# Two more tiles turned by TensorE, three small loads moved to other queues, and the instruction order searched anew

## The chip, the core and the metric

The kernel runs on one core of one Trainium2 chip. A core has five engines that run side by side and wait for each other through semaphores: TensorE (PE, matrix products and transposes), VectorE (DVE), ScalarE (ACT), GpSimd (POOL) and SyncE (SP, which here only issues transfers). Transfers between the chip's memory (HBM) and the core's memory (SBUF), and transposes inside SBUF, are carried out by 16 DMA engines; SP, ACT and POOL each feed them through a queue of their own. Products are summed in PSUM, eight banks of 512 float32 values per partition. The metric is the device time of one execution, in microseconds.

## The reference

The input x is (1, 2048, 640) in bfloat16. Two branches work on the normalised x, and both are added to x itself:

```python
x  = A_x
xn = layernorm(x)                                  # over the 640 columns, no weights
X  = rfft2(xn, axes=(-2, -1)) * (w_r + 1j * w_i)   # 2048 x 321 complex filter
A  = irfft2(X, s=(2048, 640)).astype(bfloat16)
h  = gelu(xn @ w1 + b1)                            # 640 -> 1536, tanh approximation
B  = h @ w2 + b2                                   # 1536 -> 640
return x + A + B
```

## The kernel before

The 2048 rows are held as 16 tiles of 128 rows (row 16p + c is partition p of tile c). For each tile VectorE takes statistics (`bn_stats` on two halves of 320 columns, L651; `bn_aggr`, L653), GpSimd raises the variance to the power -1/2 (L655), and VectorE normalises (L673).

The dense branch needs the normalised tile turned, with the 640 columns on the partitions. Tiles named in `BYDMA` are turned by a DMA transpose that SP issues (L680); the others by five TensorE transposes with the identity matrix (L692) into a PSUM bank, from which VectorE or ScalarE copies them to `xnT` (L547, L548). Layer one is done in seven blocks of one, one, two, two, two, four and four tiles (`BLOCKS`), each in twelve column groups of 128: five products over the 640 columns into one PSUM bank, then gelu with bias on ScalarE (L742) into `gT`. W1 is loaded in three parts that hold column groups 0 to 2, 3 to 6 and 7 to 11 (`W1P`). The bias b1 is turned to a column by one small TensorE product with the identity (L638 copies the result). Layer two is four times three column groups, each 640 wide, for each tile. For the tiles in `KEEP` it is done early: the sum is taken out of PSUM by VectorE (L911, "kps") and added to x + b2, which waits in SBUF; for the others it is done at the end, in the same PSUM bank as the last product of the filter branch ("fps").

The filter branch is a two-dimensional Fourier transform by products with tables. VectorE folds two tiles at a time (L704, L708), a product with `gtab` transforms along the rows in steps ("aps"), products with `etab` transform the width in six groups ("bps"), small 32 x 32 products with `mtab` finish the rows ("cps"), VectorE multiplies by the filter (L809 with w_r or w_i, L813 to sum), and small products with `ntab` ("dps"), DMA transposes of the result (L834) and products with `getab` ("eps") go back. VectorE unfolds (L859, L864), and a last product with `htab` is added to layer two in PSUM; VectorE adds x + b2 (L920), and SP stores the tile (L923). x + b2 is made by a ScalarE copy of b2 (L887) and a GpSimd DMA that adds x to it (L905). That DMA waits for all loads of the filter and for the transposes of x.

The filter is loaded in 18 pieces: eight direct ones and ten mirrored ones of 16, 15 or 1 rows. Two of the direct ones are issued by GpSimd.

The order of the work is written out. Every operation has a number in the order in which the program creates it, and `ORDER` lists, for each engine, the numbers in the order in which the engine runs them. Each engine runs its list strictly in order and stops at an operation whose inputs or whose buffers aren't ready. The class `Sched` replays the lists against a small model of durations (`mm_us`, `dve_us`, `LAG` and others) only to give out PSUM banks and SBUF buffers and to place the semaphores; `PRIO`, `FOLD`, `GP`, `CHAIN` and `WAVE` belong to the search that made the lists, and some of them set dependences: `WAVE` says how many of the last transposes a reload of x waits for.

At the start, TensorE runs idle products on zeros (`WARM`: 42 at once, 12 more between the first transposes and layer one). The identity is loaded by GpSimd, b1 and the first part of W1 by ScalarE, and the rest by SP.

Of the kernel before, what the change touches and what calls it, by code (L numbers as in the profile page):

```python
# [9 lines left out]
ACT = mybir.ActivationFunctionType  # L10
# [79 lines left out]

def mm_us(n):
    return max(n / 2400.0 + 0.0027, 0.0265)
# [24 lines left out]
class Pool:  # L117
# [34 lines left out]
    "sp": """8 10 14 15 16 17 18 27 50 46 24 20 19 25 23 149 151 30 45 162 164 42 28 29 38 175 177 31 188 190 36 32  # L152
26 37 33 40 41 39 217 47 34 48 49 44 219 202 43 204 35 521 522 523 520 544 545 546 51 547 570 568 569 571 595 594
593 592 621 658 648 638 612 694 675 710 720 685 730 756 765 747 782 798 791 805""",
    "pe": """7 52 112 114 115 236 230 231 120 233 118 237 234 245 246 248 249 275 276 284 285 269 270 278 279 239 242 243 240 272 266 273
# [8 lines left out]
728 760 761 754 762 745 763 785 786 787 780 792 793 788 789 794 795 796 799 800 801 802 803""",  # L164
    "act": """11 12 13 53 116 232 121 238 235 247 250 277 286 271 280 244 241 274 268 292 256 253 134 137 283 301 265 130 328 131 322 307
# [3 lines left out]
566 563 574 573 587 457 460 466 478 475 463 469 757 597 598 481 472 624 783 748 660 661 696 732 733 767""",  # L169
    "dve": """0 54 55 56 59 58 111 60 113 117 122 123 119 66 63 62 65 64 67 124 126 125 132 135 127 138 139 69 70 72 73 71  # L170
# [5 lines left out]
662 664 665 697 698 693 699 779 701 700 674 735 768 734 709 736 737 719 769 684 770 729 772 755 771 764 746 781 790 797 804""",  # L176
    "pool": """3 1 2 9 4 57 61 68 75 82 89 96 5 103 22 21 6 110 604 630 677 650 739 640 667 774 712 722 614 784 749 758
687 703""",
# [21 lines left out]
ROW_NS = {256: 26, 384: 22, 512: 27, 640: 33, 642: 70, 768: 37, 1024: 47, 1280: 56, 1600: 68, 2560: 103, 4096: 160, 10272: 750, "acc": 152}  # L200
TAIL = 0.9
LAG = 1.6
# [5 lines left out]
class Sched:  # L208
# [38 lines left out]
    def schedule(self):  # L247
        free = {e: 0.75 for e in self.engines}
        dma_free = 0.0
# [29 lines left out]
        while left:  # L279
# [38 lines left out]
            t, e, o = best  # L318
# [8 lines left out]
            if o.nbytes:  # L327
                n, size = o.rows
                ring = rings[e]
                free[e] = ring.issue_end(t, dur, n)  # L330
                done = max(t + ring.lead, free[e] - dur + ring.lead, dma_free) + n * ROW_NS[size] / 1e3
                if e == "pool" and size == 256:
                    done = t + ring.lead + 0.6
                    dma_free += n * ROW_NS[size] / 1e3
                else:
                    dma_free = done
                ring.held.append((done, n))
                o.end = done + TAIL + (LAG if 8.0 < t < 60.0 and o.engs[0][0] != "pool" and size != 256 else 0.0)
            else:
                o.end = t + dur + LAT[e]  # L340
# [98 lines left out]
BYDMA = tuple(range(4, 16))  # L439
# [3 lines left out]
PRIO = {"hps": 30.0, "gelu": 46.5, "pb": 53.0, "pc": 64.0, "filt": 77.5, "ipc": 53.5, "eps": 47.0, "fin": 46.5}  # L443
AHEAD = 1
CHAIN = "b1 b0 c00 c01 b2 c10 d01 c11 d00 b3 b4 d11 c21 d10 c20 b5 c31 d21 d20 c30 d30 d31".split()
XASPLIT = ["01 234", "01 234", "01234", "01234", "01234", "01 234", "01 23 4", "01 234"]
KEEP = (0, 2, 3, 4, 5, 6, 9, 10, 11, 14)
HOME = tuple(sorted((KEEP + tuple(c for c in range(16) if c not in KEEP))[-8:], key=lambda c: (c not in KEEP, c)))
FOLD = (1.3, 1.8, -3.7, 28.8, -1.2, 39.3, 36.8, -1.2)
GP = (-43.0, 20.0, 8.0, 14.0, -28.0, 2.0, -14.0)  # L450
G1 = 0
WAVE = (0, 4, 0, 0, 0, 1, 0, 4, 2, 2, 3, 0, 2, 1, 1, 2)
WARM = (42, 12)


def bass_parallel_sum__spectral_gfnet__dense_activation_gelu__prompt_kernel(
# [21 lines left out]
    with ExitStack() as es:  # L478
# [51 lines left out]
        def load(dst, src, buf, rows, after=(), q="sp", issue=0.46, prio=400, gate=(), late=0.0):  # L530
            return K.op([(q, 0.7 if q == "pool" else issue)], prio, lambda e, _: e.dma_start(dst, src), writes=[buf], after=after, rows=rows, gate=gate, late=late)  # L531
# [50 lines left out]
        def load_w1(j, q="sp"):  # L582
            a, b = W1P[j]
            load(view(W1, 128 * a, [[F, 5], [1, 128 * (b - a)]]), w1v[:, :, 128 * a:128 * b], B_w1s[j], (40, 256 * (b - a)), q=q)
        load_x(0, 1)
        load(ident[:], const["I"], B_id, (8, 256), q="pool", prio=96, late=1.25)
        load_x(1, 1)
        load(b1t[:], b1v, B_b1, (1, 256), q="act", prio=410)
        load_w1(0, q="act")
        K.op([("act", 1.3)], 390, lambda e, _: e.preload_act_table(ACT.Gelu_apprx_tanh), writes=[Buf("table")], gate=[K.ops[-1]])  # L590
# [372 lines left out]
```

## Time and profile before

| | |
|---|---|
| time, three runs | 149.53, 150.71, 151.38 us (median 150.71) |
| the profiled execution | 150.96 us, its span 148.9 us |
| TensorE busy | 140.9 us, 95% of the span, 1755 products recorded |
| VectorE, ScalarE, GpSimd busy | 109.0, 85.8, 23.0 us |
| DMA | 23.68 MB in 32122 packets, mean 159 GB/s |
| granted TensorE clock | 1.00 |

The span is the time from the first to the last recorded instruction of the core; what the execution takes beyond it, 2.06 us, lies around it. "Busy" is the time in which at least one instruction of the engine runs; for TensorE the ends are modelled, and some records are missing. "PEld" is the loading of the stationary operand, which overlaps the products. A row of the timeline gives start and length in microseconds, the engine, the line of the program, what is written from what, the shape and the count of merged instructions, and in brackets the idle time ahead of it with what ended it. "SPq" and "ACTq" rows are the issuing of transfers, not the transfers. The answer for one tile ends with the time from issue to landing.

### The profile page before, as it was taken

The numbers are of one execution on the slowest core, as the hardware profiler recorded it, in microseconds if no ns is written. First come the engines' busy times: TensorE is split into PE (matmuls) and PEld (weight loads), VectorE is DVE, ScalarE is ACT, GpSimd is POOL, SyncE is SP. The second block draws the span as 40 slices with busy tenths as digits, with TensorE's granted clock in tenths as the row PEclk, the third lists the DMA queues.
The fourth block names the chain that finished last, engine by engine and source line by source line (L and its number), as shares of the span: only waits on it lengthen the run. The fifth ranks groups of instructions, "written<-read, shape, count | busy, mean of one in ns | idle before, by whom it ended". The sixth has DMA issues, their size and how long they took to land.

```text
span 148.9 us, 4190 instructions
## 1 busy us (share of the span) xinstructions
PE 140.9 (95%) x1755; PEld 92.4 (62%) x1772; DVE 109.0 (73%) x232; ACT 85.8 (58%) x159; POOL 23.0 (15%) x38
## 2 busy tenths in 40 slices
PE   7599989999979999999999999999999999999993
PEld 7599979989537554436654544554447656665572
DVE  1699799999843369759945967796102999997992
ACT  3179998899957869889655442303378640350000
POOL 3302220305200027100240002020020380000000
PEclk9999999999999999999999999999999999999999
DMA  4999999898999948904939664944624099521243
GB/s 121 342 390 317 357 102 209 209 237 201 270 177 166 173 86 176 255 13 99 158 61 164 124 165 92 89 87 92 131 45 88 4 226 262 189 76 44 88 144 127
DMA packets 32122, 23.68 MB, mean 159 GB/s; under 512 B 20440, under 2 KB 28760, under 8 KB 31976
## 3 DMA queue, kind: packets, MB, share of 16 engines
q1 hardware_dynamic: 29024, 17.32, 53.2%
q0 software_dynamic: 2400, 5.61, 17.1%
q10 hardware_dynamic: 680, 0.49, 1.1%
q8 instruction: 14, 0.23, 0.7%
q14 instruction: 4, 0.03, 0.1%
HBM read 13.58 MB, written 2.62 MB: 109 GB/s over the span
## 4 chain that ended last, share of the span: by engine, by line
PE 78%; DMA 7%; SPq 5%; ACT 4%; DVE 2%; issue 2%
PE ps L536 78%; DMA X<-in_A_x_dram 7%; SPq L531 5%; ACT gT L742 2%; ACT XV L547 1%; DVE stats L651 1%; DVE T L708 1%; ACT X L887 0%; DVE T L704 0%; DVE W L920 0%; DVE mv L653 0%
## 5 line engine op out<-in xcount | busy, mean ns | idle before, releaser
L536 PE MATMUL ps<-W,gT 128*128 128x128 bf16 (+3 forms) x380 | 54.8, 292 | 2.6 <-issue 1.1
L536 PE MATMUL ps<-xnT,W 128*128 128x256 bf16 (+2 forms) x420 | 57.1, 288 | 0.0
L536 PEld LDWEIGHTS ps<-W,gT 128*128 128x128 bf16 x396 | 29.8, 98 | 24.0 <-issue 2.2
L536 PEld LDWEIGHTS ps<-xnT,W 128*128 128x128 bf16 x420 | 34.8, 98 | 15.4 <-issue 1.2
L742 ACT ACTIVATE gT<-ps,b1col 128x256 bf16<-128x256 f32 (+2 forms) x84 | 37.9, 508 | 9.2 <-PE ps L536 9.0
L651 DVE BATCH_NORM_STATS2 stats<-X 128x6 f32<-128x320 bf16 x32 | 13.9, 475 | 3.3 <-DMA X<-in_A_x_dram 3.3
L905 POOL DMA_DIRECT2D X<-in_A_x_dram x8 | 7.0, 1126 | 51.4 <-DMA Wf<-in_A_w_i_dram 15.3
L859 DVE TENSOR_TENSOR Wf<-Wf 128x960 bf16<-128x960 bf16 (+1 forms) x12 | 7.1, 595 | 9.7 <-ACT Wf L547 9.5
L547 ACT ACTIVATE Wf<-ps 128x960 bf16<-128x960 f32 (+1 forms) x9 | 7.6, 880 | 11.2 <-PE ps L536 11.0
L809 DVE TENSOR_TENSOR T<-Y,Wf 128x1288 bf16<-128x1288 bf16 x16 | 12.4, 825 | 1.3 <-ACT Y L547 1.3
L547 ACT ACTIVATE Y<-ps 128x644 bf16<-128x644 f32 x11 | 7.5, 705 | 6.4 <-PE ps L536 6.4
L547 ACT ACTIVATE XV<-ps 128x512 bf16<-128x512 f32 (+2 forms) x12 | 9.7, 830 | 2.5 <-PE ps L536 2.5
L655 POOL TENSOR_TENSOR rstd<-mv,mhalf 128x2 f32<-128x2 f32 (+1 forms) x9 | 6.3, 704 | 29.6 <-DVE mv L653 24.5
L905 POOL DMA_DIRECT2D xnT<-in_A_x_dram x8 | 7.3, 1296 | 17.4 <-DMA XV<-U 9.6
L547 ACT ACTIVATE U<-ps 128x512 bf16<-128x512 f32 (+1 forms) x10 | 3.8, 434 | 9.3 <-PE ps L536 9.3
L547 ACT ACTIVATE Xb<-ps 128x960 bf16<-128x960 f32 (+1 forms) x7 | 7.6, 1108 | 2.7 <-PE ps L536 2.7
L708 DVE TENSOR_TENSOR T<-T 128x512 bf16<-128x512 bf16 (+1 forms) x32 | 8.3, 306 | 0.1
L920 DVE TENSOR_TENSOR W<-ps,xnT 128x640 bf16<-128x640 f32 (+2 forms) x10 | 6.8, 690 | 2.1 <-PE ps L536 1.8
L548 DVE CAST Xb<-ps 128x960 bf16<-128x960 f32 (+1 forms) x5 | 5.8, 1169 | 2.8 <-PE ps L536 2.8
L536 PE MATMUL ps<-getab,XV 32*128 32x160 bf16 (+1 forms) x128 | 7.5, 241 | 0.0
L548 DVE CAST Y<-ps 128x644 bf16<-128x644 f32 x5 | 4.1, 827 | 4.4 <-PE ps L536 4.4
L536 PEld LDWEIGHTS ps<-getab,XV 32*128 32x128 bf16 (+1 forms) x128 | 6.5, 146 | 1.3
(51 smaller groups left out, 134.8 us busy)
## 6 DMA issues: line engine op xcount, KB each, us to landing
X<-in_A_x_dram POOLq DMA_DIRECT2D x8, 320.0 KB, 4.0
xnT<-in_A_x_dram POOLq DMA_DIRECT2D x8, 320.0 KB, 5.3
out_dram<-W SPq DMA_DIRECT2D x15, 160.0 KB, 1.8
X<-in_A_x_dram SPq DMA_DIRECT2D x7, 320.0 KB, 9.7
W<-in_B_w_dram SPq DMA_DIRECT2D x4, 480.0 KB, 6.2
Wf<-in_A_w_i_dram SPq DMA_DIRECT2D x6, 160.5 KB, 6.3
Wf<-in_A_w_r_dram SPq DMA_DIRECT2D x6, 160.5 KB, 5.3
W<-in_B_w_dram SPq DMA_DIRECT2D x1, 800.0 KB, 8.8
```

The lines of the kernel that those rows point to most:

```text
L531: return K.op([(q, 0.7 if q == "pool" else issue)], prio, lambda e, _: e.dma_start(dst, src), writes=[buf], after=after, rows=rows, gate=g ...
L536: ins = e.matmul(o_, lhsT=lw, rhs=rh, start=st, stop=sp_, skip_group_check=True)
L547: return e.activation(dst(), src(), ACT.Copy, scale=scale)
L548: return e.tensor_copy(dst(), src())
L651: st_op[c] = K.op([("dve", 0.393)], pr, lambda e, _, c=c, h=h: e.bn_stats(stats[:, c, 6 * h:6 * h + 6], view(X, c * D + H2 * h, [[1, H2]]) ...
L655: K.op([("pool", 0.65)], 500, lambda e, _, a=a, b=b: e.tensor_tensor(out=rstd[:, a:b], in0=mv[:, a:b, 1], in1=mhalf[:, a:b], op=ALU.pow), ...
L708: ring_ops.append(K.op([("dve", dve_us(4 * w, 2))], pr, lambda e, _, op=op, x1v=x1v, xfv=xfv, o_=o_, o0=o0, o1=o1, w=w: e.tensor_tensor(ou ...
L742: K.op([("act", act_us(128 * nt, 1))], pr + PRIO["gelu"] + GP[bi], lambda e, _, c0=c0, nt=nt, fc=fc, hps=hps: e.activation(gT[:, fc, 128 * ...
L809: filt_ops.append(K.op([("dve", dve_us(4 * KP, 2))], pr, lambda e, _, k=k, Y=Y, TB=TB, pair=pair: e.tensor_tensor(out=view(TT, TB.slot * 8 ...
L859: K.op([("dve", dve_us(320 * n, 2))], pr + 2, lambda e, _, k=k, op=op, yo=yo, y2=y2, n=n: e.tensor_tensor(out=view(Wf, Y2 + y2.slot * 3 * ...
L905: xo_ops[c] = K.op([("pool", 0.9)], 51 - c / 20, lambda e, _, c=c, xov=xov: e.dma_start(xov(0, D), xv[:, c, :], accum_op=ALU.add), reads=[ ...
L920: K.op([("dve", dve_us(w))], 95, lambda e, _, os_=os_, fps=fps, o0=o0, w=w, xov=xov, base=base: e.tensor_tensor(out=view(W1, OST + os_.slo ...
```

## The change

Tiles 4 and 5 leave `BYDMA`, so TensorE turns six tiles instead of four, and DMA ten instead of twelve. The identity is loaded through ScalarE's queue, created behind the load of the gelu table, and b1 stays on that queue; the first part of W1 goes to SP's queue, so that all three parts are issued there, behind x tiles 0 and 1. The table load no longer has to follow the first part of W1. Of the idle products there are 38 and 12. `KEEP` loses tiles 4 and 14 and gains tile 8, so that nine tiles are kept. The cost model gets a lag by time of issue and by row size instead of one figure, and the search has been run again: every list of `ORDER` is new, and with two DMA transposes gone and ten TensorE transposes and two copies added, the numbers behind 145 are shifted.

```diff
+def lag(t, size):
+    if size == 256 or size == "acc":
+        return 0.0
+    if t >= 16.0 and size in (642, 10272):
+        return 0.3
+    return ([0.0] + [v for t0, v in LAG if t >= t0])[-1]
...
-    "sp": """8 10 14 15 16 17 18 27 50 46 24 20 19 25 23 149 151 30 45 162 164 42 28 29 38 175 177 31 188 190 36 32
-26 37 33 40 41 39 217 47 34 48 49 44 219 202 43 204 35 521 522 523 520 544 545 546 51 547 570 568 569 571 595 594
+    "sp": """8 12 13 14 15 16 17 18 19 25 20 43 28 46 32 31 24 23 27 33 37 164 166 29 48 179 190 177 192 38 49 42
+30 44 40 39 203 205 219 217 36 34 35 47 26 45 41 524 523 548 522 547 545 521 546 569 572 571 50 51 570 595 596 594
...
-LAG = 1.6
+LAG = ((1.6, 1.1), (3.9, 2.8), (16.0, 1.6), (60.0, 0.0))
...
-BYDMA = tuple(range(4, 16))
+BYDMA = tuple(range(6, 16))
...
-AHEAD = 1
+AHEAD = 3
...
-KEEP = (0, 2, 3, 4, 5, 6, 9, 10, 11, 14)
+KEEP = (0, 2, 3, 5, 6, 8, 9, 10, 11)
...
-G1 = 0
-WAVE = (0, 4, 0, 0, 0, 1, 0, 4, 2, 2, 3, 0, 2, 1, 1, 2)
-WARM = (42, 12)
+G1 = 1
+WAVE = (0, 3, 0, 0, 2, 0, 0, 4, 0, 2, 0, 2, 4, 2, 2, 3)
+WARM = (38, 12)
...
-        load(ident[:], const["I"], B_id, (8, 256), q="pool", prio=96, late=1.25)
+        K.op([("act", 1.3)], 420, lambda e, _: e.preload_act_table(ACT.Gelu_apprx_tanh), writes=[Buf("table")])
+        load(ident[:], const["I"], B_id, (8, 256), q="act", prio=410)
+        load(b1t[:], b1v, B_b1, (1, 256), q="act", prio=405)
         load_x(1, 1)
-        load(b1t[:], b1v, B_b1, (1, 256), q="act", prio=410)
-        load_w1(0, q="act")
-        K.op([("act", 1.3)], 390, lambda e, _: e.preload_act_table(ACT.Gelu_apprx_tanh), writes=[Buf("table")], gate=[K.ops[-1]])
+        load_w1(0)
         load_w1(1)
```

What the new lists do, in words. SP: x tiles 0 and 1, the three parts of W1 with x tiles 2 and 3 ahead of the third, `gtab`, x tiles 4 and 5, 6 and 7, 12 and 13, 8 and 9, a filter piece, x tiles 14 and 15, three small items, x tiles 10 and 11; b2 comes behind the first part of W2, `getab` and `htab` between the last transposes. The transposes of tiles 12 to 15 stand ahead of seven last loads, among them the fourth part of W2 and two mirrored pieces of w_i. ScalarE: b1, the table load, the identity, then copies and gelus; its first copy of b2 comes behind the last eviction of the row transform. GpSimd: its two filter loads are issued between the powers of the early tiles, the first of them waiting for x tiles 6 and 7. TensorE: all 50 idle products first, then the ten transposes of tiles 0 and 1, then layer one; layer two begins behind the third group of the width transform. VectorE: one half of tile 1's statistics ahead of tile 0's mean, tile 1's normalising ahead of the copy of tile 0; the product with w_i for the first pair ahead of the copy of the third group of the width transform.

More of the change, by code (lines that the diff above doesn't have):

```diff
@@ L151 @@
 ORDER = {
[L152 to L155 removed]
[8 rows of a table removed]
[L164 to L165 removed]
[3 rows of a table removed]
[L169 to L170 removed]
[5 rows of a table removed]
[L176 to L178 removed]
+    "sp": """8 12 13 14 15 16 17 18 19 25 20 43 28 46 32 31 24 23 27 33 37 164 166 29 48 179 190 177 192 38 49 42
+30 44 40 39 203 205 219 217 36 34 35 47 26 45 41 524 523 548 522 547 545 521 546 569 572 571 50 51 570 595 596 594
+593 622 613 658 649 639 675 685 694 757 731 711 766 748 721 782 798 791 805""",
+    "pe": """115 7 52 114 112 120 118 231 234 235 270 232 237 238 273 274 271 267 268 279 280 282 283 285 286 276 243 277 240 244 241 246
[8 rows of a table added]
+709 763 776 746 777 764 719 778 792 785 779 786 787 780 788 793 789 794 795 796 799 800 801 802 803""",
+    "act": """11 9 10 116 121 53 236 233 275 272 239 269 281 284 287 278 245 242 248 251 260 293 263 296 135 254 130 299 131 132 326 323
[3 rows of a table added]
+758 568 578 577 588 592 749 482 476 473 464 467 470 783 774 479 599 625 660 661 696 697 733 734 768 769""",
+    "dve": """0 55 54 58 56 59 60 111 117 113 119 122 123 127 63 62 65 66 64 67 124 125 126 133 136 140 139 138 143 141 142 144
[5 rows of a table added]
+657 663 665 664 638 698 648 699 693 701 700 674 684 735 736 737 738 770 756 730 710 765 720 771 772 773 747 781 790 797 804""",
+    "pool": """3 1 2 57 5 61 68 21 75 6 4 22 82 89 96 103 110 605 723 631 641 677 667 703 713 740 750 615 651 687 784 775
+759""",
 }
@@ L248, in schedule @@
         free = {e: 0.75 for e in self.engines}
-        dma_free = 0.0
+        dma_free = dma_last = 0.0
         rings = {"sp": Ring(1.05, 140), "act": Ring(1.05, 140), "pool": Ring(1.7, 200)}
@@ L330, in schedule @@
                 free[e] = ring.issue_end(t, dur, n)
-                done = max(t + ring.lead, free[e] - dur + ring.lead, dma_free) + n * ROW_NS[size] / 1e3
-                if e == "pool" and size == 256:
-                    done = t + ring.lead + 0.6
+                turn = size == 256 and n == 40
+                done = max(t + ring.lead, free[e] - dur + ring.lead, dma_last if turn else dma_free) + n * ROW_NS[size] / 1e3
+                dma_last = max(dma_last, done + lag(t, size))
+                if e == "act":
+                    done = t + ring.lead + 0.5
                     dma_free += n * ROW_NS[size] / 1e3
@@ L337, in schedule @@
                 ring.held.append((done, n))
-                o.end = done + TAIL + (LAG if 8.0 < t < 60.0 and o.engs[0][0] != "pool" and size != 256 else 0.0)
+                o.end = done + TAIL + lag(t, size)
             else:
@@ L442 @@
         "eps": [(0, 4)], "fin": [(4, 8), (0, 4)], "fps": [(4, 8)], "tps": ANY, "aps": ANY}
-PRIO = {"hps": 30.0, "gelu": 46.5, "pb": 53.0, "pc": 64.0, "filt": 77.5, "ipc": 53.5, "eps": 47.0, "fin": 46.5}
-AHEAD = 1
-CHAIN = "b1 b0 c00 c01 b2 c10 d01 c11 d00 b3 b4 d11 c21 d10 c20 b5 c31 d21 d20 c30 d30 d31".split()
-XASPLIT = ["01 234", "01 234", "01234", "01234", "01234", "01 234", "01 23 4", "01 234"]
-KEEP = (0, 2, 3, 4, 5, 6, 9, 10, 11, 14)
-HOME = tuple(sorted((KEEP + tuple(c for c in range(16) if c not in KEEP))[-8:], key=lambda c: (c not in KEEP, c)))
-FOLD = (1.3, 1.8, -3.7, 28.8, -1.2, 39.3, 36.8, -1.2)
-GP = (-43.0, 20.0, 8.0, 14.0, -28.0, 2.0, -14.0)
-G1 = 0
-WAVE = (0, 4, 0, 0, 0, 1, 0, 4, 2, 2, 3, 0, 2, 1, 1, 2)
-WARM = (42, 12)
+PRIO = {"hps": 23.0, "gelu": 27.0, "pb": 67.5, "pc": 50.5, "filt": 84.0, "ipc": 36.0, "eps": 80.0, "fin": 28.5}
+AHEAD = 3
+CHAIN = "b1 b0 c01 c00 b2 c10 d01 c11 d00 b4 b3 d10 d11 c20 c21 b5 c30 d20 d21 c31 d30 d31".split()
+XASPLIT = ["01 23 4", "01234", "01234", "01234", "01234", "01234", "0123 4", "01 23 4"]
+KEEP = (0, 2, 3, 5, 6, 8, 9, 10, 11)
+HOME = tuple(sorted((KEEP + tuple(c for c in range(16) if c not in KEEP))[-8:], key=lambda c: (c not in KEEP, c)))
+FOLD = (1.3, 1.8, -3.2, 66.3, 45.3, 69.8, 50.8, 17.3)
+GP = (-81.0, 42.0, 4.0, 72.0, -32.0, 6.0, -9.0)
+G1 = 1
+WAVE = (0, 3, 0, 0, 2, 0, 0, 4, 0, 2, 0, 2, 4, 2, 2, 3)
+WARM = (38, 12)
 def bass_parallel_sum__spectral_gfnet__dense_activation_gelu__prompt_kernel(
```

32 rows, old and new, of the table ORDER are left out of this document.

## The prediction

> **What bounds the kernel now.** I read the page's shares first, then busy time by stage, then the timeline around each place where TensorE (PE) stands idle.
>
> ```profile
> span 148.9 us, 4190 instructions
> PE 140.9 (95%) x1755; PEld 92.4 (62%) x1772; DVE 109.0 (73%) x232; ACT 85.8 (58%) x159; POOL 23.0 (15%) x38
> ...
> 8.00:43.00 35.00, 33.79 (x384) 28.97 (x381) 32.66 (x106) 33.00 (x77) 6.52 (x11) 1.00 1.06 248
> 43.00:112.00 69.00, 67.67 (x973) 35.67 (x985) 43.45 (x70) 40.19 (x65) 9.63 (x11) 1.00 0.69 122
> 112.00:147.00 35.00, 34.00 (x336) 22.50 (x340) 29.43 (x46) 10.76 (x14) 4.41 (x5) 1.00 0.45 128
> ```
>
> The stage rows give window, length, then busy us of PE, PEld, DVE (VectorE), ACT (ScalarE), POOL, clock, DMA share and GB/s. PE bounds everything from its first real product to the end. From 8 to 43 us three engines are level: PE 33.8, ACT 33.0, DVE 32.7 of 35 us, and the DMA share is full. Later DVE and ACT have room. So a microsecond is won where PE stands still, or by starting earlier; and it is lost by anything put on PE. The profiled execution took 150.96 us (2.06 outside the span), 0.25 over the median of 150.71; the sum is made against 150.96.
>
> PE stands still in three places that can be named, the first of them the start:
>
> ```profile
> 0.74 0.62 ACTq L531 DMA_DIRECT2D b1t<-in_B_b_dram  x1
> 1.31 0.71 POOL L531 DMA_DIRECT2D ident<-c_I  x1 [0.34 <-issue]
> 1.83 1.28 ACT L590 ACT_TABLE_LOAD   x1 [1.83 <-issue]
> 3.15 0.89 DVE L651 BATCH_NORM_STATS2 stats<-X 128x6 f32<-128x320 bf16 x2 [2.21 <-DMA X<-in_A_x_dram]
> 4.07 0.22 DVE L653 BATCH_NORM_AGGREGATE mv<-stats 128x2 f32<-128x15 f32 x1
> 4.38 0.57 POOL L655 TENSOR_TENSOR rstd<-mv,mhalf 128x1 f32<-128x1 f32 x1 [2.22 <-DVE mv L653]
> 4.98 0.45 DVE L673 TENSOR_SCALAR T<-X,mv,rstd 128x640 bf16<-128x640 bf16 x1
> 6.53 0.18 PE L536 MATMUL ps<-ident,b1t 12*128 12x12 bf16 x1 [1.60 <-DMA ident<-c_I]
> 7.01 0.36 DVE L548 COPY xnT<-ps 128x384 bf16<-128x384 bf16 x1 [1.45 <-PE ps L692]
> 7.61 0.61 PE L536 MATMUL ps<-xnT,W 128*128 128x128 bf16 x8
> 8.50 4.09 PE L536 MATMUL ps<-xnT,W 128*128 128x128 bf16 x69
> 12.63 0.44 PE L692 MATMUL ps<-ident,T 128*128 128x128 bf16 x5
> 12.90 0.50 PE L536 MATMUL ps<-xnT,W 128*128 128x128 bf16 x6
> 18.36 1.67 DVE L651 BATCH_NORM_STATS2 stats<-X 128x6 f32<-128x320 bf16 x4 [0.96 <-DMA X<-in_A_x_dram]
> 21.97 0.45 PE L536 MATMUL ps<-gtab,T 128*128 128x128 bf16 x5 [0.38 <-DVE T L708]
> 43.27 0.70 PE L536 MATMUL ps<-W,gT 128*128 128x128 bf16 x4 [1.07 <-ACT gT L742]
> 46.39 1.31 PE L536 MATMUL ps<-etab,XV 128*128 128x160 bf16 x24
> ```
>
> Tile 0 is normalised at 4.98 + 0.45 = 5.43, but PE turns it only behind 6.53, since the identity matrix lands then; the first product of layer one runs at 7.61. At 21.97 PE waits 0.38 for a fold on DVE, which had itself waited 0.96 for x tile 6. At 43.27 the second layer's first product waits 1.07.
>
> ```profile
> 42.28 0.71 ACT L742 ACTIVATE gT<-ps,b1col 128x512 bf16<-128x512 f32 x1
> ...
> L531 SPq DMA_DIRECT2D W<-in_B_w_dram x1: 434/434/434, 36.0 to 36.0; - x1
> DMA to landing us min/median/max: 7.0/7.0/7.0
> ```
>
> Two things end there together: a gelu at 42.28 + 0.71 = 42.99, and the fourth part of W2, issued at 36.0 and landed 7.0 later, at 43.0. The product reads all of W2, so the named releaser need not be the true one.
>
> **The change part by part.**
>
> *Start: -0.7.* The identity goes from POOL's queue to ScalarE's, behind b1 and the table load. Queue time 0.74 + 0.62 = 1.36, table 1.28, so issue at about 2.65; the first x load, also a plain one, took 3.15 - 0.74 = 2.4 from issue to use, so it lands near 5.1. If the issue need not wait for the table it is 3.8; with the 5.2 that POOL's own load took (1.31 to 6.53) it is 7.9. I take 5.1, the nearest kind. Then DVE sets the start: its new order takes one half of tile 1's statistics ahead of tile 0's mean, so 3.15 + 0.89 + 0.45 + 0.22 = 4.7, POOL 0.57 to 5.3, normalise 0.45 to 5.8; tile 1's root 0.56 behind POOL's first and its normalise come ahead of tile 0's copy (0.36): 5.3 + 0.6 + 0.45 + 0.36 = 6.7, and the first product near 6.9 instead of 7.6. The twelve idle products that stood between are now ahead of the turns, where PE waits anyway.
>
> *Turns on PE: +0.28.* A tile takes 12.90 - 12.63 = 0.27 us of PE. Tiles 4 and 5 add 0.54 on the path; tile 1's 0.27 now lies ahead of 6.9 and leaves it. Bounds: +0.27, and 2 x 0.44 = 0.88 where nothing of a turn overlaps its neighbours.
>
> *Their copies: 0.* Each costs ACT 704 ns, and tile 3's copy goes to DVE.
>
> ```profile
> L547 ACT ACTIVATE xnT<-ps 128x640 bf16<-128x640 bf16 x2 | 1.3, 704 | 0.1
> L887 ACT ACTIVATE X<-b2bc 128x640 f32<-128x640 bf16 x8 | 5.8, 744 | 0.0
> xnT<-T SPq DMA_TRANSPOSE x12, 4.9
> ```
>
> That is +1.4 - 0.7 on ACT in its full stage, but the new order also moves three copies of b2 (744 ns each) from before the last stage-one eviction to behind it: 0.7 - 2.2 is negative. DVE gets five thirds of the 0.36 that a copy of three fifths takes, 0.6, and loses the 0.96 wait. Uncovered, these would cost 0.7. SP loses two transposes with 4.9 us to landing each; they are not missed on PE unless the next item is late.
>
> *x in another order: -0.4.* Tile 6 now follows tile 4 in SP's queue, so the wait of 0.96 goes and with it PE's 0.38. b2 and the last stage's table (getab) no longer stand before it. Next late would be tile 5's copy, which stands on ACT behind tile 4's; were it the last to end, it would cost up to its 0.7.
>
> *Second layer: -1.07.* Its first product moves behind the third group of the width transform, some ten microseconds, past both candidates. What PE does instead is layer one for tiles 8 to 11, whose transposes then are wanted earlier; their normalisations come sooner by 0.7 + 0.96 - 0.6 = 1.1, which covers it.
>
> *W1 in three parts by SP: +0.3.* Seven of twelve column blocks need parts one and two: 70 products for tiles 0 and 1, at 4.09/69 = 59 ns, 4.1 us. Starting at 6.9, PE asks for part three at 11.0.
>
> ```profile
> L531 SPq DMA_DIRECT2D W<-in_B_w_dram x1: 512/512/512, 2.7 to 2.7; - x1
> DMA to landing us min/median/max: 8.8/8.8/8.8
> 5.00:10.00 5.00, 3.47 (x61) 3.43 (x62) 3.29 (x10) 2.31 (x9) 0.56 (x1) 1.00 1.06 376
> ```
>
> It landed at 2.7 + 8.8 = 11.5, and the engines were full (share 1.06). With the same bytes ahead of it the wait is 0.5; if one queue spreads the sixteen engines less, 0; issued one issue (0.5) later with the same 8.8, 1.0. I take 0.3. The Trainium skill ("DMA: Bandwidth & Descriptors", section on issuing engines not being separate queues) says that all queues run on the same 16 engines and a second issuer saves issue time alone; by that rule part three comes no sooner and the term is 0.5, the forecast 0.2 later.
>
> *POOL, SP's late loads, KEEP: 0.* POOL's first filter load now waits for x tile 6 ahead of the root of tiles 4 and 5; were tile 6 late, these and PE would be.
>
> ```profile
> 96.85 1.28 SPq L834 DMA_TRANSPOSE XV<-gtab  x1
> 103.35 2.52 SPq L834 DMA_TRANSPOSE XV<-T  x2
> ```
>
> getab and htab are now issued ahead of the last five of these transposes; SP was free from 98.1 to 103.35 there, and two issues of about 0.5 fit. Nine tiles instead of ten keep a partial sum: one DVE add less, in a stage with 29.4 of 35 us. The second layer's products stay the same in number.
>
> *The new order's own small waits: +0.5.* The order puts DVE's chains flush with PE's cover in the middle (both halves of one 960-wide eviction on DVE). Bounds: 0 where each cover holds, and 2, half as much again as the 69.0 - 67.67 = 1.3 that the middle loses now.
>
> Sum: -0.7 + 0.28 - 0.38 - 1.07 + 0.3 + 0.5 = -1.07: 150.96 - 1.07 = **149.9 us**.
>
> **The rivals.**
>
> *The start is given back.* If part three of W1 takes 0.8 and the small waits 0.8, the sum is -0.27 and the two waits removed are just replaced: 150.7. For it: the share of 1.06. Against: less competes with part one.
>
> *It doesn't do what it says: the identity is late.* From 5.8, where tile 0 is normalised, each microsecond of the identity costs one. At 6.5, as now, the start's 0.7 is gone: 150.6; at 7.9, the upper bound, 2.1: 152.0. For it: the table load stands ahead of the issue. Against: 0.7 lie between 5.1 and 5.8. The Trainium skill ("ScalarE: Activation LUTs", section on what the table load costs) gives 1283 ns, which the row of 1.28 confirms, and a drain of 1380 ns behind it, which no row here shows; by its 2.66 the issue is at 4.0, the landing at 6.4, and the time 150.5, an estimate.
>
> *Slower: the last filter rows are late.* In the new order DVE's product with the imaginary filter stands ahead of the copy of the third width group (in the old one behind it).
>
> ```profile
> 17.07 3.90 SPq L680 DMA_TRANSPOSE xnT<-T  x2
> ...
> 39.93 1.44 SPq L680 DMA_TRANSPOSE xnT<-T  x1
> ...
> 50.79 0.59 SPq L531 DMA_DIRECT2D Wf<-in_A_w_i_dram  x1
> DMA to landing us min/median/max: 3.7/3.7/3.7
> ...
> 56.64 1.24 DVE L548 CAST Xb<-ps 128x960 bf16<-128x960 f32 x1
> 57.77 1.56 DVE L809 TENSOR_TENSOR T<-Y,Wf 128x1288 bf16<-128x1288 bf16 x2
> ...
> 58.70 0.49 PE L536 MATMUL ps<-Xb,mtab 32*32 32x322 bf16 x32
> ```
>
> Queued behind a late product are that copy, PE's small products that read it (58.70), and, PE being in order, everything. Until now the last rows landed at 50.8 + 3.7 = 54.5 against a use at 57.8. Now SP issues seven loads behind the last four transposes. If all four start near 40, as tile 14's did, at 1.44 each they end at 45.8, and seven loads of 0.59 at 49.9; 3.7 to 7.0 later is 53.6 to 56.9. The point from which it decides: the small products at 58.7 want the copy (1.24) and the filter product (0.78) done, so rows by 56.7; beyond it each microsecond costs one, and 1.1 make it slower than before. At 1.95 a transpose, as the first two took, the rows land up to 2.0 later, 58.9: 149.9 + 2.2 = 152.1. Against it: two transposes fewer stand in the queue.
>
> *More goes than I count.* With ACT 1.5 us lighter in the full stage, the small waits of PE there vanish too, and the middle keeps its pace: 0.5 becomes -1, so 148.4.
>
> **How the numbers follow.** Forecast 0.5; start given back 0.13; identity late 0.07; slower 0.16; more 0.14. Range 147.9 to 152.8: the lower end is the last case with half a microsecond, the upper leaves out the worst half of the slower one. The likeliest case alone spans 149.0 to 150.9. Two per cent of 150.71 is 3.0 us, about what a measurement of this kernel tells from no change: faster needs under 147.7 (half of the last case and a little more, 0.11), slower over 153.7 (beyond the slow case's end, and what no row shows, 0.13), within 0.76.
>
> **What would show it.** Right: first product of layer one near 6.9 with the identity in by 5.5; ten turns on PE before it; no wait for DVE near 22 and none for W2; the first product with etab starting about 1 us earlier than 46.39; last filter rows before 56.7. Wrong: a PE wait of over 0.6 for W1, DVE waiting for filter rows, DVE stopping in the statistics for tiles 8 or 10, or new PE waits of over 1 us behind 56.

## The result, and the profile after

The changed kernel takes 149.75 us (median of 22 runs, 149.32 to 150.33) against 150.67 for the kernel before (22 runs, most of them between 149.5 and 151.9). The ratio of the two is 0.994, with a 95% interval of 0.9921 to 0.9959: faster by 0.9 us, far less than 2%. Medians here are over all runs of a kernel, while the ratios, each to the kernel before measured beside it, leave out single runs that lie over 1.5% above their kernel's fastest. The profiled execution took 149.76 us with a span of 147.8, so 1.20 less than the profiled execution of before.

The page's shares, then the busy time of the stage in which TensorE had stood still, with the columns of the prediction:

```profile
span 147.8 us, 4200 instructions
PE 142.2 (96%) x1760; PEld 93.9 (64%) x1778; DVE 108.5 (73%) x230; ACT 86.5 (59%) x161; POOL 22.6 (15%) x37
```

```profile
8.00:43.00 35.00, 34.93 (x392) 29.59 (x390) 33.01 (x107) 31.28 (x71) 6.66 (x11) 1.00 1.03 242
```

From 8 to 43 us TensorE now stands still for 0.07 instead of 1.21. Both waits are gone, 0.38 near 22 and 1.07 near 43. What is behind them is as long as it was. The first product with `etab` and the last product of all in after, then the last product in before:

```profile
45.23 1.31 PE L546 MATMUL ps<-etab,XV 128*128 128x160 bf16 x24
...
145.12 0.23 PE L546 MATMUL ps<-Wf,htab 128*128 128x160 bf16 x1
```

```profile
146.29 0.23 PE L536 MATMUL ps<-Wf,htab 128*128 128x160 bf16 x1
```

From the first of these products to the last it is 99.89 us in after and 99.90 in before (146.29 less 46.39). So the whole gain is made before the first product with `etab`, which comes 1.16 earlier. The longest wait that TensorE still has behind its first product, from the view of waits (total, times, longest):

```profile
PE ps L702 <- ACT xnT L557: 0.2, 1, 0.2
```

The start, by the timeline of after:

```profile
0.99 5.52 PE L546 MATMUL ps<-warm 128*128 128x128 bf16 x50 [0.99 <-DVE warm L562]
1.39 1.28 ACT L596 ACT_TABLE_LOAD   x1 [1.39 <-PEq L958]
1.42 0.36 ACTq L541 DMA_DIRECT2D ident<-c_I  x1
...
5.15 0.45 DVE L683 TENSOR_SCALAR T<-X,mv,rstd 128x640 bf16<-128x640 bf16 x1
...
6.44 0.19 PE L546 MATMUL ps<-ident,b1t 12*128 12x12 bf16 x1
...
7.61 5.56 PE L546 MATMUL ps<-xnT,W 128*128 128x128 bf16 x88
```

```profile
L541 ACTq DMA_DIRECT2D ident<-c_I x1: 364/364/364, 1.4 to 1.4; - x1
DMA to landing us min/median/max: 2.4/2.4/2.4
```

The identity is issued at 1.42, beside the table load and not behind it, and lands at 3.8. Tile 0 is normalised at 5.6. Yet TensorE's first use of the identity is at 6.44, since the 50 idle products hold TensorE until 6.4, and layer one begins at 7.61, exactly as before.

### The profile page after: what moved, and what is told of

Its sections match the earlier page's. It is cut to its first block, busy times and chain, and to the rows that moved or that the text cites. A ratio compares the mean times of both kernels' runs of the same rounds, so it can differ in the third digit from the quotient of the medians.

```text
span 147.8 us, 4200 instructions
## 1 busy us (share of the span) xinstructions
PE 142.2 (96%) x1760; PEld 93.9 (64%) x1778; DVE 108.5 (73%) x230; ACT 86.5 (59%) x161; POOL 22.6 (15%) x37
## 4 chain that ended last, share of the span: by engine, by line
PE 94%; ACT 2%; issue 2%; DVE 0%
PE ps L546 93%; ACT gT L752 1%; PE ps L702 1%; ACT Y L557 0%; ACT xnT L557 0%; DVE W L930 0%; DVE warm L562 0%
## 5 line engine op out<-in xcount | busy, mean ns | idle before, releaser
L546 PE MATMUL ps<-xnT,W 128*128 128x256 bf16 (+2 forms) x420 | 57.8, 288 | 0.1
L557 ACT ACTIVATE Wf<-ps 128x960 bf16<-128x960 f32 (+1 forms) x10 | 8.5, 888 | 13.5 <-PE ps L546 13.5
L819 DVE TENSOR_TENSOR T<-Y,Wf 128x1288 bf16<-128x1288 bf16 x16 | 12.5, 822 | 0.5 <-ACT Y L557 0.4
L558 DVE CAST Xb<-ps 128x960 bf16<-128x960 f32 (+1 forms) x7 | 7.9, 1141 | 3.9 <-PE ps L546 3.9
L558 DVE CAST Wf<-ps 128x640 bf16<-128x640 f32 (+1 forms) x2 | 2.0, 991 | 10.8 <-PE ps L546 10.8
L557 ACT ACTIVATE XV<-ps 128x1280 bf16<-128x1280 f32 (+3 forms) x10 | 9.3, 946 | 0.8 <-PE ps L546 0.8
L718 DVE TENSOR_TENSOR T<-T 128x128 bf16<-128x128 bf16 (+1 forms) x32 | 8.4, 308 | 0.1
L557 ACT ACTIVATE U<-ps 128x512 bf16<-128x512 f32 (+1 forms) x8 | 3.1, 434 | 7.5 <-PE ps L546 7.5
L921 DVE TENSOR_TENSOR X<-ps,X 128x640 f32<-128x640 f32 x8 | 6.5, 817 | 1.2 <-PE ps L546 1.2
L714 DVE TENSOR_TENSOR T<-T 128x640 bf16<-128x640 bf16 x16 | 7.2, 479 | 0.1
## 6 DMA issues: line engine op xcount, KB each, us to landing
X<-in_A_x_dram SPq DMA_DIRECT2D x7, 320.0 KB, 11.1
```

Of the source, the lines that this page charges most:

```text
L546: ins = e.matmul(o_, lhsT=lw, rhs=rh, start=st, stop=sp_, skip_group_check=True)
L557: return e.activation(dst(), src(), ACT.Copy, scale=scale)
L558: return e.tensor_copy(dst(), src())
L714: K.op([("dve", dve_us(640, 2))], pr, lambda e, _, k=k, op=op, xnv=xnv, x1v=x1v: e.tensor_tensor(out=x1v(H2 * k, [[D, 2], [1, H2]]), in0=x ...
L718: ring_ops.append(K.op([("dve", dve_us(4 * w, 2))], pr, lambda e, _, op=op, x1v=x1v, xfv=xfv, o_=o_, o0=o0, o1=o1, w=w: e.tensor_tensor(ou ...
L819: filt_ops.append(K.op([("dve", dve_us(4 * KP, 2))], pr, lambda e, _, k=k, Y=Y, TB=TB, pair=pair: e.tensor_tensor(out=view(TT, TB.slot * 8 ...
```

## The experiments

**Fewer idle products.**

```diff
-WARM = (38, 12)
+WARM = (31, 12)
```

> The changed kernel with 43 idle products ahead of the turns instead of 50. Theory A, the idle products hold the start: in the profiled execution they ran at 0.107 us each until 6.4, while tile 0 was normalised at 5.6 and the identity had landed at 3.8. Seven fewer end 0.75 earlier, the turns start near 5.8, the first product of layer one near 6.9 instead of 7.6, and the time falls by 0.6 to about 149.1. Rival B, VectorE, which is busy without a break from 16 to 36 us, is the second bound: the first product comes at 6.9 all the same, but TensorE waits for VectorE or ScalarE later by as much, and the time stays at 149.6 to 149.8. Rival C, the identity or the first part of W1 holds the start: the first product stays at 7.6.

Measured: 149.79 us (12 runs), ratio 0.9935 (0.9912 to 0.9957), no different from the changed kernel. TensorE's timeline of this kernel, and the issue and landing of W1's third part:

```profile
0.99 4.54 PE L546 MATMUL ps<-warm 128*128 128x128 bf16 x43 [0.99 <-DVE warm L562]
...
6.59 4.52 PE L546 MATMUL ps<-xnT,W 128*128 128x128 bf16 x70
11.65 1.56 PE L546 MATMUL ps<-xnT,W 128*128 128x128 bf16 x25 [0.54 <-ACT gT L752]
```

```profile
L541 SPq DMA_DIRECT2D W<-in_B_w_dram x1: 433/433/433, 3.4 to 3.4; - x1
DMA to landing us min/median/max: 8.1/8.1/8.1
```

The first half of theory A holds: the idle products had held the turns, and layer one begins 1.0 us earlier. The pace of the products doubles at some point of the start (last section), here at 5.1 and in the profile of after at 6.8. The last kernel of this section, with all 50 idle products and the same start, has this step at 4.9 and begins layer one at 6.83, so only a part of the 1.0 is due to the seven products fewer. The second half doesn't hold: 0.54 is lost waiting for the third part of W1, which lands at 3.4 + 8.1 = 11.5 (the row names a gelu; the product also waits for this part and runs 0.14 behind its landing). Having begun at 6.59, TensorE asks for the part at 11.1; having begun at 7.6 it asks near 12.1, when the part is there. Of the three theories none had this, though rival B's time came out; it is the prediction's own term for W1, paid only when the start is early. VectorE's timeline near the end:

```profile
144.27 1.09 DVE L930 TENSOR_TENSOR W<-ps,xnT 128x320 bf16<-128x320 f32 x3 [0.55 <-DMA out_dram<-W]
```

TensorE's last product still starts 0.35 earlier than in after (144.77 against 145.12). This does not reach the end in this execution: the additions before the last stores wait 0.55 for an earlier store, the last store is issued at 145.9 against 145.7, and the span is 147.9 against 147.8. Whether the other runs lose it in the same way no trace here shows.

```diff
-WARM = (38, 12)
+WARM = (18, 12)
```

> The changed kernel with 30 idle products instead of 50. At 0.107 us each they end at 4.2, and TensorE stands idle until tile 0 is normalised at 5.6. Theory A, only the length of the idle products matters: like 43 of them, first product near 6.8, time 149.1. Rival D, the step from 0.107 to 0.055 us a product, which came at 4.0 in the profile of before and at 6.8 in that of after, needs TensorE busy over a stretch of some 3 us before it: the 1.4 us of standing idle put it off, the first products of layer one run at 0.107 for up to 3.4 us more, and the time rises by up to 1.7, to 150 to 151.5, with more spread than the 1.0 us of the changed kernel.

Measured: 150.88 us, ratio 1.0026 (1.0002 to 1.005), 1.1 above the changed kernel. TensorE's timeline, one microsecond of the windows, and the last stores:

```profile
6.86 6.88 PE L546 MATMUL ps<-xnT,W 128*128 128x128 bf16 x95
```

```profile
8.00:9.00 1.00, 1.00 (x13) 1.00 (x11) 0.60 (x3) 0.69 (x2) 0.00 (x0) 1.00 1.05 374
```

```profile
L933 SPq DMA_DIRECT2D out_dram<-W x9: 332/425/1352, 137.9 to 146.7; - x9
```

Rival D's mechanism holds. The first product is at 6.86, but only eleven weight loads fall into the microsecond, one every 0.107 us where one every 0.056 is full pace, and this goes on to about 9.1. In the thirteen other profiles of this case the step to full pace lay between 4.0 and 6.8. The granted clock column stays at 1.00 all the while; the pace is read from the loads alone. The price is another matter. In this execution TensorE's last product starts only 0.17 later than in after (145.29 against 145.12). About 0.8 of the 1.0 us that the execution takes longer comes behind it, where the issue of one store holds SyncE for 1.35 us (the longest of the last nine issues in after took 0.46). Why all twelve runs take 150.3 or more is therefore open.

**The identity back on GpSimd's queue.**

```diff
-        load(ident[:], const["I"], B_id, (8, 256), q="act", prio=410)
+        load(ident[:], const["I"], B_id, (8, 256), q="pool", prio=96)
```

> The changed kernel with the identity back on GpSimd's queue. Theory A, the idle products hold the turns until 6.4: the identity lands near 6.5 as in before, TensorE turns at 6.5 to 6.6, and the time rises by 0 to 0.2, to 149.8 to 149.9. The prediction's own step, the identity sets the start and its move is worth 0.7: time 150.4, and the first product of layer one near 8.2.

Measured: 149.80 us, ratio 0.9955 (0.993 to 0.9979). The identity's issue and landing here:

```profile
L541 POOL DMA_DIRECT2D ident<-c_I x1: 709/709/709, 1.3 to 1.3; - x1
DMA to landing us min/median/max: 3.4/3.4/3.4
```

Theory A's time holds: the move of the identity is worth nothing here. Its landing does not: 4.7 and not 6.5, though the queue and the issue are those of before. In the five profiles that have the start of before it landed between 5.5 and 6.5, so the spread alone hardly explains it. What differs nearby is that the first part of W1 isn't on ScalarE's queue; that this is the cause is argued, not shown.

**The queues alone, on the kernel before.** The identity goes to ScalarE's queue, behind the table load, and the first part of W1 to SyncE's (behind x tile 1 in SyncE's list); the table load no longer has to follow that part; the rest is as before.

```diff
-        load(ident[:], const["I"], B_id, (8, 256), q="pool", prio=96, late=1.25)
+        load(ident[:], const["I"], B_id, (8, 256), q="act", prio=410)
...
-        load_w1(0, q="act")
-        K.op([("act", 1.3)], 390, lambda e, _: e.preload_act_table(ACT.Gelu_apprx_tanh), writes=[Buf("table")], gate=[K.ops[-1]])
+        load_w1(0)
+        K.op([("act", 1.3)], 390, lambda e, _: e.preload_act_table(ACT.Gelu_apprx_tanh), writes=[Buf("table")])
```

> The kernel before with nothing but the identity on ScalarE's queue and the first part of W1 on SyncE's, each engine's order kept otherwise. If the queues alone are worth the start's 0.7 and more: identity in at 3.8, turns at 5.5 behind the 42 idle products, first product at 6.6 instead of 7.58, time 149.7. Rival, the order of layer one must come with it: the fourth column group of tile 0, 1.1 us behind the first product, needs part two of W1, which lands near 8.2, so TensorE waits some 0.5 there and the time is 150.2. Second rival, what is won is lost at the fold near 22 or at the second layer's first product, both of which wait for transfers: time 150.7, and those waits longer by what was won.

Measured: 150.40 us, ratio 0.999 (0.996 to 1.0019): no gain that shows. Timeline of TensorE, then parts one and two of W1, then the fourth part of W2 and the two stretches:

```profile
7.25 0.61 PE L536 MATMUL ps<-xnT,W 128*128 128x128 bf16 x8 [0.38 <-DMA W<-in_B_w_dram]
9.10 4.08 PE L536 MATMUL ps<-xnT,W 128*128 128x128 bf16 x65 [0.57 <-ACT gT L742]
```

```profile
L531 SPq DMA_DIRECT2D W<-in_B_w_dram x2: 434/480/526, 1.7 to 2.1; - x2
DMA to landing us min/median/max: 5.5/6.1/6.8
```

```profile
L531 SPq DMA_DIRECT2D W<-in_B_w_dram x1: 433/433/433, 35.7 to 35.7; - x1
DMA to landing us min/median/max: 5.9/5.9/5.9
```

```profile
20.00:24.00 4.00, 4.00 (x51) 3.72 (x50) 3.89 (x14) 4.00 (x10) 0.88 (x1) 1.00 0.73 162
40.00:44.00 4.00, 3.95 (x35) 2.45 (x35) 2.27 (x8) 3.03 (x6) 0.00 (x0) 1.00 1.13 196
```

The first rival holds for the start: TensorE waits for part one (7.1) and for part two (2.1 + 6.8 = 8.9; the row names a gelu, and the product runs 0.14 behind this landing, as the one at 7.25 does behind that of part one). The order of layer one, tiles 0 and 1 in turn, belongs with the queues. What nobody expected: in this execution (149.9) both waits of the middle are absent. The fourth part of W2, with nothing changed about it, was issued 0.3 earlier than in the profile of before and landed 1.4 earlier, at 41.6. So that wait can be absent without any of the moves below.

**The two waits alone, on the kernel before.** The fourth part of W2 (26) directly behind the transposes of tiles 8 to 11:

```diff
-    "sp": """8 10 14 15 16 17 18 27 50 46 24 20 19 25 23 149 151 30 45 162 164 42 28 29 38 175 177 31 188 190 36 32
-26 37 33 40 41 39 217 47 34 48 49 44 219 202 43 204 35 521 522 523 520 544 545 546 51 547 570 568 569 571 595 594
+    "sp": """8 10 14 15 16 17 18 27 50 46 24 20 19 25 23 149 151 30 45 162 164 42 28 29 38 175 177 31 188 190 26 36
+32 37 33 40 41 39 217 47 34 48 49 44 219 202 43 204 35 521 522 523 520 544 545 546 51 547 570 568 569 571 595 594
```

> The kernel before with one move in SyncE's list: the fourth part of W2 is issued directly behind the transposes of tiles 8 to 11, ahead of a filter piece and the table mtab, so 1.3 us earlier and ahead of GpSimd's two filter pieces. Theory A, the landing of this part (42.97 in the profile of before) is what the second layer's first product waited for, and since it competes with GpSimd's two pieces it comes now early, now late, which makes the spread of before: the part lands by 41, the product starts at 41.8 without a wait, median 149.6 to 149.9, spread under 1 us. Rival B, the gelu that the profile names as releaser (ended 42.99): the wait of about 1 us stays and the median stays at 150.6.

x tile 6 (19, one load for tiles 6 and 7) ahead of tiles 10 and 8 (24, 20):

```diff
-    "sp": """8 10 14 15 16 17 18 27 50 46 24 20 19 25 23 149 151 30 45 162 164 42 28 29 38 175 177 31 188 190 36 32
+    "sp": """8 10 14 15 16 17 18 27 50 46 19 24 20 25 23 149 151 30 45 162 164 42 28 29 38 175 177 31 188 190 36 32
```

> The kernel before with x tile 6 loaded ahead of tiles 10 and 8 in SyncE's list. It lands 1.6 us earlier, near 16.7, so VectorE loses its wait of 0.96 and TensorE its 0.38 at the fold near 22. Theory A, as the prediction has it, the 0.38 is won: median 150.2 to 150.3. Rival B, it only arrives earlier at the second layer's first product, which waits for the landing of W2, so the wait there grows from 1.07 to 1.45 and the median stays at 150.6.

Both moves:

> The kernel before with both moves, W2's fourth part behind the transposes of tiles 8 to 11 and x tile 6 ahead of tiles 10 and 8. If the two waits of 0.38 and 1.07 are the whole of what the change won, this has 150.96 - 1.45 = 149.5 in a profiled execution and a median of 149.2 to 149.6, at or below the changed kernel's 149.75, with neither its turns nor its queues. If the middle of the kernel (VectorE full from 20 to 36 us) takes up a part, 149.8 to 150.2.

Measured: W2 early 149.99 us, ratio 0.9947 (0.9915 to 0.998); x tile 6 early 149.48 in six runs, 0.9886 (0.9847 to 0.9924); both 149.65, 0.9949 (0.9909 to 0.9989). With W2 early, its fourth part, then the first product of layer one and that of the second layer, and ScalarE's gelu there:

```profile
L531 SPq DMA_DIRECT2D W<-in_B_w_dram x1: 581/581/581, 35.3 to 35.3; - x1
DMA to landing us min/median/max: 4.9/4.9/4.9
```

```profile
8.29 0.61 PE L536 MATMUL ps<-xnT,W 128*128 128x128 bf16 x8 [1.29 <-DMA W<-in_B_w_dram]
42.25 1.52 PE L536 MATMUL ps<-W,gT 128*128 128x128 bf16 x10
42.28 0.71 ACT L742 ACTIVATE gT<-ps,b1col 128x512 bf16<-128x512 f32 x1
```

With x tile 6 early, the same part and the two stretches:

```profile
L531 SPq DMA_DIRECT2D W<-in_B_w_dram x1: 434/434/434, 35.6 to 35.6; - x1
DMA to landing us min/median/max: 5.6/5.6/5.6
```

```profile
20.00:24.00 4.00, 4.00 (x49) 3.70 (x47) 3.89 (x12) 4.00 (x10) 0.88 (x1) 1.00 0.82 145
40.00:44.00 4.00, 3.95 (x40) 2.58 (x39) 1.64 (x7) 2.56 (x6) 0.00 (x0) 1.00 1.15 205
```

With W2 landed at 40.2 the second layer's first product runs at 42.25, while the gelu that had been named runs from 42.28 to 42.99: the landing and not the gelu had been the releaser. So theory A of the first kernel holds for the wait; its median is just above the range, and its runs still spread by 2.0 (149.3 to 151.4), so W2's landing alone does not make the spread of before. The same profile shows what the start is worth in the old order: layer one began 0.68 later than in before, at 8.29, and TensorE still ended what precedes the second layer at 42.2, as in before. For x tile 6 neither theory was right. VectorE's 0.96 and TensorE's 0.38 go, and W2, issued 0.4 earlier, comes early as well; this profiled execution took 149.42. That the earlier issue is what brings W2 in time is not shown: in the profile of the repeat below it is issued at 36.0, as in before, lands at 41.5, and the product doesn't wait either. Both moves together took 149.43 in the profiled execution, the 149.5 of their expectation, so the two waits are the whole of what the profile of before loses.

Since six runs are few, the same kernel was run again beside the changed one, and once with the queues added:

> The changed kernel itself once more, beside the three others of this group. Median 149.6 to 149.9, first product of layer one between 6.7 (where the idle products reach 0.055 us early) and 7.6, no wait over 0.2 between 9 and 50. If the kernel before with x tile 6 early is as fast as this within 0.3 us, the turns, the queues, the later second layer and the new lists are together worth no more than one place in SyncE's list.

> The kernel before with x tile 6 ahead of tiles 10 and 8, in the same group as the changed kernel. Theory A, the earlier result of 149.48 stands, since VectorE's earlier chain also lets SyncE issue W2's fourth part 0.4 earlier, and it landed at 41.2, ahead of the product at 41.3: median 149.4 to 149.8. Rival B, six runs were luck: W2 still lands late in part of the executions, median 150.0 to 150.4, with a spread like that of before.

> The kernel before with x tile 6 early, the identity on ScalarE's queue and the first part of W1 on SyncE's. Theory A, the start is bound by the stream of W1 (part two landed at 8.4 to 9.0, part three at 11.3 to 12.0 in all profiles, whatever the queue), so the queues give nothing beyond x tile 6: 149.4 to 149.8. Rival B, they give the 0.4 by which the first product came earlier with the queues alone: 149.0.

Measured in one group: the changed kernel 149.50 (ratio 0.9943, 0.9913 to 0.9973), x tile 6 early 150.32 (0.9967, 0.9928 to 1.0006), x tile 6 and the queues 151.11 (1.001, 0.9968 to 1.0053). The fastest runs are near each other (149.08, 149.37, 149.46), and the profiled executions, all near their fastest, show neither wait. Higher up the kernels differ: the changed one stays under 150.6, the other two spread beyond 151. So rival B of the second kernel holds this time and theory A held the first time, and no theory of the third kernel gave its median, which is 150.42 without its three slowest runs. In the three profiles of the old order with x tile 6 early, layer one begins at 7.71, 7.30 and, with the queues, 6.98, and they take 149.42, 149.48 and 149.46: there an earlier start wins nothing. In the changed kernel it does, as the next section tells. One load moved by two places is enough for an execution without either wait; that the median stays low needs more of the change. Which landing is late in the slower runs no trace here shows.

**Tiles 4 and 5 turned by DMA again.** Their two transposes are issued in SyncE's free time; their turns and copies are left out and the numbers behind them shifted, the lists kept otherwise (not shown here).

```diff
-BYDMA = tuple(range(6, 16))
+BYDMA = tuple(range(4, 16))
```

> The changed kernel with tiles 4 and 5 turned by DMA as before, the two transposes at the place in SyncE's list where it is free (between 14.8 and 22), their TensorE turns and copies left out, the rest of the order kept. Theory A, TensorE's turns cost 0.54 and buy an earlier start of layer one on these tiles: normalised at 18.9 and 19.25, with the 4.4 to 4.9 us from issue to landing that before's transposes took, and 1.3 for each issue, the turned tiles are there at 23 and 24.3, while TensorE asks for them at 22.1: a wait of 1 to 2 near 22, median 150.3 to 151.2. Rival B, the products of tiles 4 and 5 are covered by other work as before: the time falls by the 0.5 of turns, to 149.2.

Measured: 158.52 us, ratio 1.0477 (1.0437 to 1.0517). The two transposes in before and here, then TensorE's timeline and windows here:

```profile
L680 SPq DMA_TRANSPOSE xnT<-T x2: 1322/1924/2527, 17.1 to 18.4; - x2
...
DMA to landing us min/median/max: 4.4/4.7/4.9
```

```profile
L690 SPq DMA_TRANSPOSE xnT<-T x2: 1320/1527/1734, 19.5 to 20.9; - x2
DMA to landing us min/median/max: 6.6/6.9/7.3
```

```profile
28.24 9.66 PE L546 MATMUL ps<-xnT,W 128*128 128x256 bf16 x68 [5.17 <-DMA xnT<-T]
```

```profile
28.00:33.00 5.00, 4.76 (x25) 3.50 (x26) 4.77 (x17) 1.25 (x3) 0.69 (x1) 0.55 1.03 233
33.00:38.00 5.00, 5.00 (x50) 4.45 (x49) 2.81 (x8) 3.65 (x10) 0.00 (x0) 1.00 0.68 156
```

Theory A's direction, at many times its price. The transposes land 6.6 to 7.3 us after issue instead of 4.4 to 4.9; that they stand behind the loads that the new order has put ahead is the likely reason, not a shown one. TensorE stands still for 5.17 us, and then runs with a granted clock of 0.55 until 33 (25 products in 5 us against 50 in the next 5). In the new lists, with the transposes at this place, the two turned tiles are not a saving but a need.

**x tile 6 late in the changed kernel** (19 behind 25 and 20):

```diff
-    "sp": """8 12 13 14 15 16 17 18 19 25 20 43 28 46 32 31 24 23 27 33 37 164 166 29 48 179 190 177 192 38 49 42
+    "sp": """8 12 13 14 15 16 17 18 25 20 19 43 28 46 32 31 24 23 27 33 37 164 166 29 48 179 190 177 192 38 49 42
```

> The changed kernel with x tile 6 loaded behind tiles 12 and 8, so that it lands near 18.0 to 18.3 as in before instead of 15.1. Theory A, the place of x tile 6 is what the change lives on: VectorE asks for it at 17.3 and GpSimd's filter load in front of the power of tiles 4 and 5 waits for it too, so these tiles are normalised 0.7 to 1.5 later, TensorE, which turns them itself at 19.3, stands by as long, and the median is 150.3 to 151.2, as slow as before. Rival B, the new order covers it: below 150.0.

Measured: 150.90 us, ratio 1.0023 (0.9991 to 1.0056). VectorE's and TensorE's timelines:

```profile
18.04 1.28 DVE L661 BATCH_NORM_STATS2 stats<-X 128x6 f32<-128x320 bf16 x3 [1.00 <-DMA X<-in_A_x_dram]
19.79 0.80 DVE L683 TENSOR_SCALAR T<-X,mv,rstd 128x640 bf16<-128x640 bf16 x2 [0.47 <-POOL rstd L665]
```

```profile
20.29 0.45 PE L702 MATMUL ps<-ident,T 128*128 128x128 bf16 x5 [1.06 <-DVE T L683]
```

Theory A holds: 1.00 on VectorE, another 0.47 behind GpSimd, 1.06 on TensorE, and with that the whole gain is gone.

## The prediction, step by step

The forecast was 149.9, with 0.76 for a change within 2%; measured 149.75, a change of 0.6%. The sum was -1.07 in the profiled execution and came out at -1.20, but three terms were wrong and cancelled: -0.7, +0.3 and +0.5 were each 0.0. That the number is so near is luck; the two waits and the turns were understood. Of the signs, the identity was in by 5.5, the ten turns were ahead, both waits were gone and the first product with `etab` came 1.16 earlier; only the start near 6.9 failed.

- **Start, -0.7: failed.** Measured 0.0 (7.61 against 7.61). The step that failed is "the twelve idle products that stood between are now ahead of the turns, where PE waits anyway". All 50 are ahead, 5.52 us of them, and they end behind the point at which tile 0 is ready (5.6). The prediction gave them no length. At the pace of before, with the step at 4.0, they would have ended near 5.3 (28 at 0.107 and 22 at 0.056), in time; with the step at 6.8 they did not. The repeat of the changed kernel began layer one at 7.19 (its row stands in the last section) and took 149.35, 0.41 less, and the kernel with x tile 6 late began it at 6.83. So the term is there in some executions, in part or whole, and it goes with the step, which differs between executions of the same program. The identity itself did better than forecast, 3.8 against 5.1, as its issue does not wait for the table load; that was the lower bound. The Trainium skill ("ScalarE: Activation LUTs", section on what the table load costs) gives 2.66 us for the load with its drain; an issue that waits for both would by this estimate have been at 4.0. Here it is at 1.42, so neither holds this queue.
- **Turns, +0.28: consistent, not measured alone.** With the two waits it gives -1.17, and TensorE's last product comes 1.17 earlier. The kernel without them shows what the prediction did not see, that the new load order needs them.
- **Copies, 0: right.** No wait for a copy over 0.2 shows on TensorE.
- **x in another order, -0.38: right, and larger in other ways than it was told.** Late again it costs 1.1 to 1.4 (150.90 against 149.75 and 149.50); early in the kernel before it takes the 0.38 away as forecast, while whether it also brings W2 forward is open.
- **Second layer, -1.07: right** against this profile of before, and the doubt about the named releaser too. In an execution without the wait, such as that of the queues alone, the term is nothing.
- **W1, +0.3: 0.0.** It hung on a start at 6.9. With fewer idle products the start is 6.59 and the wait 0.54. The rule of the Trainium skill quoted there (that another issuer brings no more engines) agrees: part three lands between 11.1 and 12.5 where SyncE issues all three parts, and between 11.1 and 11.5 where ScalarE issues the first.
- **Small waits, +0.5: 0.0**, by the 99.9 us that are the same in both. The 1.3 from which the upper bound was made counts 0.27 of the wait for W2 again (43.00 to 43.27), and most of the rest are gaps of 0.16, of which the repeat of the changed kernel shows none (69.00 busy of 69).

Two rivals fell clearly. The identity was not late. The last filter rows, issued up to 47.6, landed up to 4.9 later, so by 52.5, against the 56.7 from which they would have cost:

```profile
L541 SPq DMA_DIRECT2D Wf<-in_A_w_i_dram x3: 589/606/1368, 45.0 to 47.6; - x3
DMA to landing us min/median/max: 4.0/4.2/4.9
```

"The start is given back" was right about the start and wrong about the waits: it put the price on W1 and on small waits, where it lay with the idle products.

## What to carry to other kernels

Work that only fills time at the start of a kernel must be priced at the pace it really runs at, and its end compared with the moment the first real input is ready: here 50 idle products hid a faster load where the pace stepped late, and with 30 layer one began at half pace. An earlier start wins only where nothing behind it waits for something else: in the old order it won nothing. Where the profile names a releaser that ended at the same time as a landing, move the landing in the queue to see which it was. A wait that is there in one execution and absent in another is worth more in the median and the spread than in the fastest run: the fastest runs here differ by 0.2, the medians by 0.9.

## What the hardware showed that was not expected

Idle products began at one every 0.107 us and stepped to one every 0.056 at a time that differed between executions of the same code, and the first product of layer one moved with it. The idle products of the changed kernel's repeat and its first product of layer one (the rows of the first profile stand in the section on the result):

```profile
0.99 5.21 PE L546 MATMUL ps<-warm 128*128 128x128 bf16 x50 [0.99 <-DVE warm L562]
7.19 5.96 PE L546 MATMUL ps<-xnT,W 128*128 128x128 bf16 x95
```

The repeat needed 5.21 us for its 50, the first profile 5.52. By the starts of the loads the step lay at 4.0 in before, at 6.8 and 5.7 in the two profiles of the changed kernel, at 4.9 in it with x tile 6 late, and near 9.1 with 30 idle products, where TensorE had stood still for 1.2 us until 5.7. The Trainium skill ("TensorE: Matmul & The Clock Gate") has a free-running activity window of 3413 ns (section on what is actually happening) and paces of 106.7 and 55.6 ns (section on 56 ns and not 53.3). Both paces agree with these traces, and steps that move between executions fit a window that doesn't begin with the kernel. In before the step came 3.0 us behind the first idle product, less than one window; how busy a window has to be no run here shows.
